# The last product of a three-stage kernel by seven products in two phases, with wider operand preparation in the stage before it

## The chip, the core and the metric

The kernel runs on one core of a Trainium2 chip. The metric is its time in microseconds of the device; the reported time is the median of three runs. The five engines of a core run programs of their own and wait for each other by semaphores: TensorE (PE) multiplies into PSUM, VectorE (DVE) and ScalarE (ACT) do elementwise work, GpSimd (POOL) has next to nothing to do here, and SyncE (SP) issues the DMA transfers.

## The reference

All values are float32. Attention without a softmax makes 4608 rows of 512, and two MLPs follow, the second with a gate:

```python
kv = einsum('bhsd,bhse->bhde', k, v); a = einsum('bhsd,bhde->bhse', q, kv)
x = a / sqrt(mean(a * a) + 1e-6) * g_norm       # 4608 x 512
h = x @ w_in                                     # 512 x 2048
x1 = (h * clip(h + 3, 0, 6) / 6) @ w_out         # 2048 x 512
g = x1 @ w_gate; val = x1 @ w_val                # 512 x 1536 each
out = (g * sigmoid(g) * val) @ w_out2            # 1536 x 512
```

## The kernel before

To keep the precision of float32, each operand of a matmul is split into a hi and a lo part (ACT copies hi, line 107; DVE subtracts to get lo, line 108), and each product is three matmuls: hi x lo, lo x hi and hi x hi. Which of the three comes first matters below: `product` (line 651) begins with the lo part of the activations.

The work comes in stages. Attention and the first MLP take the first half of the time and leave x1 in DRAM. The **gate and value stage** goes over x1 in 6 blocks of 768 tokens, twice: first with one half of the weight columns, block 0 to 5, and then with the other half, block 5 to 0. These are 12 visits, and ten times the next visit has another block. A visit has 3 steps, and a step has one quad for the gate and one for the value (`quad`), each computing a pair of column tiles for 768 tokens by seven products (a scheme of the Strassen kind) in place of eight: the activations come in as seven operands, T1, T3, B11, T2, B22, T4 and B21 in the order in which a quad uses them, B.. a quarter of the block of x and T.. a sum of quarters. Each product is 6 matmuls of 384 columns, a quad 42. The seven operands of a block are made by `prepare_x` during the last step of the visit before, from the block `xr`, loaded one visit ahead: first the sums T, then each operand's hi and lo on ACT and DVE. `gv_step` ends with the multiplication of gate and value on DVE (line 686) and a store of the result to g2d in DRAM.

Also on DVE are the sums of a quad's products (lines 668 to 677, named h1, h0 and h), which follow PE closely, since PE's accumulators in PSUM are used again. In this stage weights of later use are decoded too: w_out2 comes in as pairs of 32-bit words that `decode_w` turns into float32 (one ACT and three DVE instructions per tile), and `combine` makes the seven weight operands of a pair of tiles.

The **last product** goes over 9 blocks of 512 tokens. For each of the 12 tiles of 128 rows of w_out2 it loads a piece of g2d, splits it (`load_g2`), and multiplies it: 4 groups of 128 tokens x 3 matmuls of 512 columns (`o2_step`, lines 111 to 113). At a block's end the four accumulators are copied out and stored.

PE's program runs in the order of the code. For ACT, DVE and SP a scheduler arranges the instructions when the kernel is built; once built, each engine's sequence is fixed, and an instruction that waits holds everything behind it on its engine.

Of the kernel before, what the change touches and what calls it, by code (L numbers as in the profile page):

```python
# [18 lines left out]
def kernel(  # L19
# [579 lines left out]
    xo_slot = [0]  # L599

    def x_op(name):

        n = 6 if xo_slot[0] % 14 < 6 else 8
        pool = big["x" if n == 6 else "x2"]
        xo_slot[0] += 1
        return pool.tile([P, 2, TH], F32R, tag="xo", bufs=n, name=name)

    def prepare_x(j, x, pool=None):

        b11, b12 = x[:, 0:2, :TH], x[:, 0:2, TH:]  # L610
        b21, b22 = x[:, 2:4, :TH], x[:, 2:4, TH:]
        ops, ts = {}, {}

        def sums(*what):
            for kk in range(2):
                for key, a, b in what:
                    if pool is None or key == "T4":
                        t = w_slot(f"{key}_{j}_{kk}", F32).rearrange("p k f -> p (k f)")[:, :TH]
                    else:
                        t = pool.tile([P, TH], F32, tag="f", name=f"{key}_{j}_{kk}")  # L620
                    a_, b_ = (ts[o, kk] if isinstance(o, str) else o[:, kk] for o in (a, b))
                    nc.vector.tensor_tensor(out=t, in0=a_, in1=b_, op=ALU.subtract)
                    ts[key, kk] = t
# [406 lines left out]
```

## Time and profile before

| | |
|---|---|
| median of 3 runs | 1722.76 us (1721.68 to 1723.73) |
| profiled execution, span of its instructions | 1719.0 us |
| gate and value stage | 886.26 to 1419.56 us |
| last product | 1419.56 to 1715.0 us |
| PE busy over the span | 1688.9 us (98%) |
| DVE busy | 1185.0 us (69%) |
| ACT busy | 773.3 us (45%) |

The profile is of one execution. Its span, first to last instruction, is the part of the time that rows can be read from; the runs' times have a few microseconds more around it. A busy time is the union of an engine's instructions; a matmul's own time (0.39 us for 512 columns) is longer than the distance to the next, since they overlap, so matmuls are counted by the distance of their starts.

### The profile page before, as it was taken

The page shows a single profiled execution, that of the slowest core. Times are in us where ns is not written, and L with a number is a line of the kernel's source. Part 1 is how long each engine was busy: PE and PEld are TensorE (multiplying, and loading weights), DVE is VectorE, ACT ScalarE, POOL GpSimd, SP SyncE. Part 2 cuts the span into 40 slices and gives each one's busy share as a digit, 9 for nine tenths or more (in the row PEclk, how much of TensorE's full clock was granted, in tenths as well). Part 3 has the DMA queues.
Part 4 walks back from the last instruction along what each step waited for, and adds up shares of the span by engine and source line. Part 5 has one row for each costly group of instructions (what it writes and reads, how often), then busy time and mean ns, then how long its engine had stood idle before and what let it go on. Part 6 is the DMA issues. An engine that isn't in the chain of part 4 may idle for free.

```text
span 1719.0 us, 25593 instructions
## 1 busy us (share of the span) xinstructions
PE 1688.9 (98%) x9636; PEld 1493.1 (87%) x9636; DVE 1185.0 (69%) x2353; ACT 773.3 (45%) x1439; POOL 2.4 (0%) x7
## 2 busy tenths in 40 slices
PE   7999999999999999999999999999999999999999
PEld 3566789898898899998889999999999997888887
DVE  5897987778777777777889888777666685322321
ACT  4565554445444454545555444434443453222221
POOL 0000000000000000000000000000000000000000
PEclk8999999999999999999999999999999999999999
DMA  7886444454545444325465544572222235334332
GB/s 191 248 259 188 130 138 128 146 149 115 160 127 159 126 148 131 123 99 184 151 205 178 198 147 149 184 260 76 81 91 92 92 135 182 125 111 143 140 110 74
DMA packets 200171, 252.29 MB, mean 147 GB/s; under 512 B 79984, under 2 KB 129136, under 8 KB 200048
## 3 DMA queue, kind: packets, MB, share of 16 engines
q1 hardware_dynamic: 200048, 250.67, 45.0%
q8 instruction: 75, 1.23, 0.3%
q14 instruction: 48, 0.39, 0.1%
HBM read 185.86 MB, written 64.75 MB: 146 GB/s over the span
## 4 chain that ended last, share of the span: by engine, by line
PE 86%; DVE 8%; ACT 2%; DMA 2%; issue 1%; SPq 0%; DVEq 0%; ACTq 0%
PE q_g L651 14%; PE q_v L651 14%; PE acc L111 12%; PE acc L112 12%; PE acc L113 12%; PE a L651 6%; PE d L651 4%; PE c L651 4%; PE h L117 3%; PE kv L250 1%; DMA raw_g<-in_moe_w_gate_dram 1%; DVE lT L108 1%; DVE g L108 1%; DVE t L580 1%; PE at L112 0%
## 5 line engine op out<-in xcount | busy, mean ns | idle before, releaser
L111 PE MATMUL acc<-g,wo 128*128 128x512 f32 x512 | 202.1, 395 | 0.0
L112 PE MATMUL acc<-g,wo 128*128 128x512 f32 x512 | 199.9, 390 | 0.0
L113 PE MATMUL acc<-g,wo 128*128 128x512 f32 x512 | 199.5, 390 | 0.0
L108 DVE TENSOR_TENSOR g2l<-g,g2h 128x512 fp32r<-128x512 f32 x108 | 73.4, 692 | 139.1 <-ACT g2h L107 138.5
L111 PE MATMUL acc<-wl,g2h 128*128 128x512 f32 x432 | 168.2, 389 | 1.0 <-ACT g2h L107 1.0
L112 PE MATMUL acc<-wh,g2l 128*128 128x512 f32 x432 | 168.2, 389 | 0.3 <-DVE g2l L108 0.3
L113 PE MATMUL acc<-wh,g2h 128*128 128x512 f32 x432 | 168.1, 389 | 0.0
L579 ACT ACTIVATE t<-h,three 128x512 f32<-128x512 f32 x120 | 86.7, 722 | 138.8 <-DVE h L574 109.5
L107 ACT ACTIVATE g2h<-g 128x512 fp32r<-128x512 f32 x108 | 67.9, 632 | 147.7 <-PE acc L112 74.3
L107 ACT ACTIVATE g<-t 128x512 fp32r<-128x512 f32 x144 | 90.9, 631 | 88.8 <-DVE t L580 73.6
L108 DVE TENSOR_TENSOR g<-t,g 128x512 fp32r<-128x512 f32 x144 | 97.9, 680 | 31.6 <-ACT g L107 31.2
L113 PEld LDWEIGHTS acc<-g,wo 128*128 128x128 f32 x512 | 96.1, 188 | 20.5
L111 PEld LDWEIGHTS acc<-g,wo 128*128 128x128 f32 x512 | 96.2, 188 | 19.9
L112 PEld LDWEIGHTS acc<-g,wo 128*128 128x128 f32 x512 | 96.2, 188 | 18.3
L111 PEld LDWEIGHTS acc<-wl,g2h 128*128 128x128 f32 x432 | 81.1, 188 | 18.0 <-ACT g2h L107 1.4
L112 PEld LDWEIGHTS acc<-wh,g2l 128*128 128x128 f32 x432 | 81.1, 188 | 17.5 <-DVE g2l L108 0.6
L580 DVE SCALAR_TENSOR_TENSOR t<-t,h 128x512 f32<-128x512 f32 x120 | 82.6, 688 | 19.3 <-ACT t L579 15.7
L113 PEld LDWEIGHTS acc<-wh,g2h 128*128 128x128 f32 x432 | 81.1, 188 | 16.9
L117 PE MATMUL h<-x,w_i 128*128 128x512 f32 x192 | 87.0, 602 | 1.9 <-DVE w_i L170 1.9
L117 PEld LDWEIGHTS h<-x,w_i 128*128 128x128 f32 x192 | 36.7, 193 | 43.2 <-issue 40.2
L651 PE MATMUL q_v<-hT,v 128*128 128x384 f32 x288 | 73.6, 336 | 0.0
L679 ACT ACTIVATE hg<-q_g 128x384 f32<-128x384 f32 x36 | 17.6, 490 | 113.3 <-PE q_g L651 113.3
(245 smaller groups left out, 4483.3 us busy)
## 6 DMA issues: line engine op xcount, KB each, us to landing
wo<-wod SPq DMA_DIRECT2D x128, 512.0 KB, 3.4
g2d<-hv SPq DMA_DIRECT2D x36, 768.0 KB, 3.4
g<-g2d SPq DMA_DIRECT2D x108, 256.0 KB, 4.6
xr<-x1d SPq DMA_DIRECT2D x11, 1536.0 KB, 6.7
x1d<-x1o SPq DMA_DIRECT2D x36, 256.0 KB, 2.9
out_dram<-o SPq DMA_DIRECT2D x36, 256.0 KB, 2.1
raw_i<-in_moe_w_in_dram SPq DMA_DIRECT2D x16, 512.0 KB, 5.3
raw_o<-in_moe_w_out_dram SPq DMA_DIRECT2D x16, 512.0 KB, 4.4
```

Source lines behind the costliest of these rows:

```text
L107: nc.scalar.activation(out=hi, in_=src, func=AF.Copy)
L108: nc.vector.tensor_tensor(out=lo, in0=src, in1=f32(hi), op=ALU.subtract)
L111: nc.tensor.matmul(out_, wh, xl, start=start, stop=False)
L112: nc.tensor.matmul(out_, wl, xh, start=False, stop=False)
L113: nc.tensor.matmul(out_, wh, xh, start=False, stop=stop)
L117: nc.tensor.matmul(out_, f32(w), f32(x), start=start, stop=stop)
L250: nc.tensor.matmul(ps[h * D:(h + 1) * D, :D], kt[:, h, r, :], vt[:, h, r, :], start=i == 0, stop=i == len(steps) - 1,)
L579: nc.scalar.activation(out=t, in_=h[i], func=AF.Relu, bias=three[:, 0:1])
L580: nc.vector.scalar_tensor_tensor(out=t, in0=t, scalar=6.0, in1=h[i], op0=ALU.min, op1=ALU.mult)
L651: nc.tensor.matmul(ps, a[:, kk], b[:, kk], start=first and n == 0, stop=n == 5, skip_group_check=True,)
L679: nc.scalar.activation(out=h[:, 0], in_=a, func=AF.Copy)
```

## The change

It has three parts. The last product is now done by the scheme of seven products, too: per block of 512 tokens the 12 tiles of w_out2 make 6 pairs, and each pair needs seven products of 6 matmuls with 256 columns (`g_product`). A block has two phases: in the first (`o2_one`) all six pairs do the four products with T1, T3, B11 and T2, in the second (`o2_two`) the three with B22, T4 and B21. The operands of g2 are made for two pairs at once, in instructions of 512 and 1024 elements (`g_one` for the first phase, `g_two` for the second); B11 and B12's data are thus loaded once for the first phase, B21 and B22 twice.

The weights' seven operands per pair are made during the second half of the gate and value stage, one half pair per step in steps 18 to 29, written to DRAM and loaded again near its end.

In the gate and value stage the operands of x are prepared in wider instructions: T1, T3 and T4 each in one piece of 768 elements, B11 with T2 in one of 1536 and B21 with B22 in another. T2 is formed in place, from T3 and B11, in the block's own tile.

```diff
-    def prepare_x(j, x, pool=None):
-        b11, b12 = x[:, 0:2, :TH], x[:, 0:2, TH:]
-        b21, b22 = x[:, 2:4, :TH], x[:, 2:4, TH:]
...
-        def splits(*what):
-            for key, src in what:
-                hi, lo = x_op(f"h{key}_{j}"), x_op(f"l{key}_{j}")
-                if src is not None:
-                    split(hi, lo, src)
-                else:
-                    for kk in range(2):
-                        split(hi[:, kk], lo[:, kk], ts[key, kk])
-                ops[key] = hi, lo
-        sums(("T1", b12, b11), ("T3", b22, b12))
-        if pool is None:
-            sums(("T2", b22, "T1"), ("T4", "T2", b21))
-        splits(("T1", None), ("T3", None), ("B11", b11))
-        if pool is not None:
-            sums(("T2", b22, "T1"))
...
         yield ops
-        if pool is not None:
-            sums(("T4", "T2", b21))
-        splits(("T2", None), ("B22", b22), ("T4", None), ("B21", b21))
...
+        pair = xo_pair("x2", "B1", T2, "0")
+        for c in (slice(0, TH), slice(TH, T2)):
+            split(pair[0][:, :, c], pair[1][:, :, c], x[:, 0:2, c])
+        ops.update(halves_of(pair, "B11", "T2"))
+        yield from prepare_rest(0, x, ops)
...
+    def prepare_rest(j, x, ops):
+        t = big["xt"].tile([P, 2, TH], F32, tag="t", name=f"T4_{j}")
+        nc.vector.tensor_tensor(out=t, in0=x[:, 0:2, TH:], in1=x[:, 2:4, :TH], op=ALU.subtract)
+        pair = xo_pair("x2", "B2", T2, str(j))
+        split(pair[0], pair[1], x[:, 2:4])
+        ops.update(halves_of(pair, "B21", "B22"))
+        hi, lo = xo_pair("x", "T4", TH, str(j))
+        split(hi, lo, t)
+        ops["T4"] = hi, lo
         yield ops
+    def prepare_x(j, x):
+        ops = {}
+        b11, b12, b22 = x[:, 0:2, :TH], x[:, 0:2, TH:], x[:, 2:4, TH:]
+        t = big["xt"].tile([P, 2, TH], F32, tag="t", name=f"T1_{j}")
+        nc.vector.tensor_tensor(out=t, in0=b12, in1=b11, op=ALU.subtract)
+        nc.vector.tensor_tensor(out=b12, in0=b22, in1=b12, op=ALU.subtract)
+        for key, src in (("T1", t), ("T3", b12)):
+            hi, lo = xo_pair("x", key, TH, str(j))
+            split(hi, lo, src)
+            ops[key] = hi, lo
+        nc.vector.tensor_tensor(out=b12, in0=b12, in1=b11, op=ALU.add)
+        pair = xo_pair("x2", "B1", T2, str(j))
+        split(pair[0], pair[1], x[:, 0:2])
+        ops.update(halves_of(pair, "B11", "T2"))
+        yield from prepare_rest(j, x, ops)
...
+    def flat(o):
+        return o.rearrange("p k f -> p (k f)")
+    def w2_operands(q, tiles):
+        w2[q] = {
+            key: tuple(flat(o) for o in ops) for key, ops in operands(tiles).items()
+        }
+    def g2_rows(f0, n, r0):
+        return g2d[f0:f0 + n, :, r0:r0 + TO].rearrange("f p t -> p f t")
+    g_ops, t4s = {}, {}
...
+    def g_one(j, u):
+        n = f"{j}_{u}"
+        raw = big["gr"].tile([P, 2, 2, TO], F32, tag="raw", name=f"graw_{n}")
+        nc.sync.dma_start(
+            out=raw.rearrange("p q f t -> p (q f) t"), in_=g2_rows(4 * u, 4, j * TO)
+        )
+        t13 = big["gt"].tile([P, 2, 2, TO2], F32, tag="t13", name=f"gt13_{n}")
+        t4 = t4s[j, u] = slot(f"t4_{n}").rearrange("p (n c) -> p n c", n=2)
+        sub(
+            t13, raw[:, :, :, TO2:],
+            raw[:, :, 0].rearrange("p q (b t) -> p q b t", b=2),
+        )
+        b12 = raw[:, :, 0, TO2:]
+        sub(b12, raw[:, :, 1, TO2:], t13[:, :, 0])
+        sub(t4, b12, raw[:, :, 1, :TO2])
+        hi, lo = (
+            big["gx"].tile([P, 2, 4, TO2], F32R, tag=f"x{o}", name=f"gx{o}_{n}") for o in "hl"
+        )
+        split(hi[:, :, 0:2], lo[:, :, 0:2], t13)
+        split(
+            hi[:, :, 2:4].rearrange("p q b t -> p q (b t)"),
+            lo[:, :, 2:4].rearrange("p q b t -> p q (b t)"), raw[:, :, 0],
...
+    def g_two(j, u):
+        n = f"{j}_{u}"
+        raws_ = [slot(f"gb_{n}_{i}") for i in range(2)]
+        for i, r in enumerate(raws_):
+            nc.sync.dma_start(out=r, in_=g2d[4 * u + 2 * i + 1, :, j * TO:(j + 1) * TO])
+        hi, lo = (
+            big["gy"].tile([P, 2, 3, TO2], F32R, tag=f"y{o}", name=f"gy{o}_{n}") for o in "hl"
+        )
+        split(hi[:, :, 2], lo[:, :, 2], t4s.pop((j, u)))
+        for i, r in enumerate(raws_):
+            split(
+                hi[:, i, 0:2].rearrange("p b t -> p (b t)"),
+                lo[:, i, 0:2].rearrange("p b t -> p (b t)"), r,
+            )
...
+    def g_product(ps, g, w, first):
+        for i in range(TO2 // P):
             cs = slice(i * P, (i + 1) * P)
-            mm3(
-                ps[i], g[0][:, cs], g[1][:, cs],
-                w2[f][0].rearrange("p k f -> p (k f)"), w2[f][1].rearrange("p k f -> p (k f)"),
-                f == 0, f == NF2 - 1,
-            )
-        if f < NF2 - 1:
+            for n, (a, b) in enumerate(((g[0], w[1]), (g[1], w[0]), (g[0], w[0]))):
+                nc.tensor.matmul(
+                    ps[:, i * TO2:(i + 1) * TO2], a[:, cs], b,
+                    start=first and i == 0 and n == 0, stop=n == 2, skip_group_check=True,
+                )
...
+    def o2_one(j, q):
+        if q == 0:
+            for i, k in enumerate("aecd"):
+                acc2[k] = big["ps"].tile([P, 512], F32, tag=f"q{i}", name=f"o2{k}_{j}")
+        for k, b, a in (
+            ("c", "T1", "S1"), ("d", "T3", "S3"), ("a", "B11", "A11"), ("e", "T2", "S2"),
+        ):
+            g_product(acc2[k], g_ops.pop((j, q, b)), w2[q][a], q == 0)
+        if q < NQ - 1:
             return
...
+        acc2["u"], acc2["v"] = slot(f"u_{j}"), slot(f"v_{j}")
+        for o, p, r in (("v", "c", "d"), ("u", "a", "e")):
+            nc.scalar.activation(out=acc2[o], in_=acc2[p], func=AF.Copy)
+            nc.vector.tensor_tensor(out=acc2[o], in0=acc2[o], in1=acc2[r], op=ALU.add)
...
+    def o2_two(j, q):
+        for k, b, a in (("c", "B22", "S4"), ("d", "T4", "A22"), ("a", "B21", "A12")):
+            g_product(acc2[k], g_ops.pop((j, q, b)), w2[q][a], False)
+        if q == 0:
+            o = slot("o")
+            nc.vector.tensor_tensor(out=o, in0=acc2["u"], in1=acc2["v"], op=ALU.add)
+            put(j, o, 1, 1)
+        if q < NQ - 1:
+            return
+        for k, dm, tok in (("c", 0, 1), ("d", 1, 0)):
+            o = slot("o")
+            nc.vector.tensor_tensor(out=o, in0=acc2["u"], in1=acc2[k], op=ALU.add)
+            put(j, o, dm, tok)
+        o = slot("o")
+        nc.scalar.activation(out=o, in_=acc2["a"], func=AF.Copy)
+        put(j, o, 0, 0)
...
-                f = c - NB2 * NH
-                last = {15: (4, 5, 6), 16: (7, 8), 17: (9, 10, 11)}
-                for f in last.get(f, (f,) if f < 4 else ()):
-                    w2[f] = split_w(load_w2nd("2", f), f"2{f}")
-            if c == len(steps) - 2:
-                g2 = {m: load_g2(*order2[m]) for m in range(G_FIRST)}
...
-        for c in range(len(order2) + G_AHEAD):
-            if G_FIRST <= c < len(order2):
-                g2[c] = load_g2(*order2[c])
-            if c >= G_AHEAD:
-                j, f = order2[c - G_AHEAD]
-                if f == 0:
-                    acc2 = [
-                        big["ps"].tile([P, 512], F32, tag=f"q{i}", name=f"acc2_{j}_{i}")
-                        for i in range(TO // P)
-                    ]
-                o2_step(j, f, g2.pop(c - G_AHEAD), acc2)
...
+                m = c - NB2 * NH
+                if m < W2_STEPS:
+                    tiles = make_w2(m // 2, m % 2)
+                    if tiles:
+                        for k, t in enumerate(tiles):
+                            nc.sync.dma_start(out=w2d[m // 2, k], in_=flat(f32(t)))
+            m = c - len(steps)
+            if m == -3:
+                reload_w2(0)
+                g_first(JO[0], 0)
+            elif m == -2:
+                reload_w2(1)
+                g_first(JO[0], 1)
+            elif m == -1:
+                reload_w2(2)
+                reload_w2(3)
...
+        units = [(j, h, u) for j in JO for h in range(2) for u in range(NQ // 2)]
+        def prepare_g(n):
+            if 0 < n < len(units):
+                j, h, u = units[n]
+                (g_two if h else g_one)(j, u)
+        prepare_g(1)
+        reload_w2(4)
+        reload_w2(5)
+        for n, (j, h, u) in enumerate(units):
+            prepare_g(n + 2)
+            for q in (2 * u, 2 * u + 1):
+                (o2_two if h else o2_one)(j, q)
 
```

The first place is the change of blocks in the gate and value stage on DVE: here block 3 is made ready during the last value quad of block 2's first visit. lT, lB are the lo parts of the sums T and of the quarters B, hv the value quad's result, the xr and T rows in the second fence the sums T2 and T4. Before, from the quad's first sum on:

```order
L668 TENSOR_TENSOR h1v_11280<-h1v_11280,q_v_11284 128x384
L108 TENSOR_TENSOR lT_3_11354<-T_3_0_11337,hT_3_11353 128x384
L108 TENSOR_TENSOR lT_3_11354<-T_3_1_11341,hT_3_11353 128x384
L108 TENSOR_TENSOR lT_3_11360<-T_3_0_11339,hT_3_11359 128x384
L672 TENSOR_TENSOR h0v_11279<-h0v_11279,q_v_11282 128x384
L108 TENSOR_TENSOR lT_3_11360<-T_3_1_11343,hT_3_11359 128x384
L675 TENSOR_TENSOR hv_11278<-h1v_11280,h0v_11279 128x384
L676 TENSOR_TENSOR hv_11278<-h0v_11279,q_v_11283 128x384
L108 TENSOR_TENSOR lB_3_11366<-xr_10942,hB_3_11365 128x768
L677 TENSOR_TENSOR hv_11278<-h0v_11279,q_v_11284 128x384
L108 TENSOR_TENSOR lT_3_11370<-T_3_0_11345,hT_3_11369 128x384
L686 TENSOR_TENSOR hv_11278<-hg_11220,hv_11278 128x1536
```

The same place after the change:

```order
L691 TENSOR_TENSOR h1v_11219<-h1v_11219,q_v_11223 128x384
L110 TENSOR_TENSOR lT_3_11280<-T_3_11276,hT_3_11279 128x768
L110 TENSOR_TENSOR lT_3_11284<-xr_10881,hT_3_11283 128x768
L695 TENSOR_TENSOR h0v_11218<-h0v_11218,q_v_11221 128x384
L664 TENSOR_TENSOR xr_10881<-xr_10881 128x2x384
L698 TENSOR_TENSOR hv_11217<-h1v_11219,h0v_11218 128x384
L699 TENSOR_TENSOR hv_11217<-h0v_11218,q_v_11222 128x384
L700 TENSOR_TENSOR hv_11217<-h0v_11218,q_v_11223 128x384
L644 TENSOR_TENSOR T_3_11292<-xr_10881 128x768
L709 TENSOR_TENSOR hv_11217<-hg_11159,hv_11217 128x1536
L110 TENSOR_TENSOR lB_3_11289<-xr_10881,hB_3_11288 128x1536
L110 TENSOR_TENSOR lB_3_11295<-xr_10881,hB_3_11294 128x1536
```

The lo part of B11 stood between two of the quad's sums and ahead of the multiplication; the lo of B11 and T2, now one instruction of 1536 elements, stands behind T2's sum, T4's sum and the multiplication. (Two pairs of lB follow each other in this piece of the program; the first is B11 with T2.)

On ACT at the same place the hi parts (hT, hB) are made, between copies of accumulators (h1v, h0v, hv). Before:

```order
L667 ACTIVATE h1v_11280<-q_v_11283 128x384
L107 ACTIVATE hT_3_11353<-T_3_0_11337 128x384
L107 ACTIVATE hT_3_11353<-T_3_1_11341 128x384
L107 ACTIVATE hT_3_11359<-T_3_0_11339 128x384
L670 ACTIVATE h0v_11279<-q_v_11281 128x384
L107 ACTIVATE hT_3_11359<-T_3_1_11343 128x384
L107 ACTIVATE hB_3_11365<-xr_10942 128x768
```

After:

```order
L690 ACTIVATE h1v_11219<-q_v_11222 128x384
L109 ACTIVATE hT_3_11279<-T_3_11276 128x768
L109 ACTIVATE hT_3_11283<-xr_10881 128x768
L693 ACTIVATE h0v_11218<-q_v_11220 128x384
L109 ACTIVATE hB_3_11288<-xr_10881 128x1536
L702 ACTIVATE hv_11217<-q_v_11220 128x384
L109 ACTIVATE hB_3_11294<-xr_10881 128x1536
```

Four hi parts of 384 elements became two of 768, and B11's copy of 768 elements became one of 1536 that needs T2's sum from DVE.

On PE a block of the last product begins as follows, acc being the four accumulators and g2h, g2l the split rows of g2. Before:

```order
L111 MATMUL acc_4_0_16229<-wl_12866,g2h_0_16069 128x512
L112 MATMUL acc_4_0_16229<-wh_12865,g2l_0_16070 128x512
L113 MATMUL acc_4_0_16229<-wh_12865,g2h_0_16069 128x512
L111 MATMUL acc_4_1_16230<-wl_12866,g2h_0_16069 128x512
L112 MATMUL acc_4_1_16230<-wh_12865,g2l_0_16070 128x512
L113 MATMUL acc_4_1_16230<-wh_12865,g2h_0_16069 128x512
```

After (o2c is one of four accumulators, gxh and gxl hold the operands of two pairs):

```order
L815 MATMUL o2c_16311<-20_3_14867,gxh_0_16196 128x256
L815 MATMUL o2c_16311<-20_2_14866,gxl_0_16197 128x256
L815 MATMUL o2c_16311<-20_2_14866,gxh_0_16196 128x256
L815 MATMUL o2c_16311<-20_3_14867,gxh_0_16196 128x256
L815 MATMUL o2c_16311<-20_2_14866,gxl_0_16197 128x256
L815 MATMUL o2c_16311<-20_2_14866,gxh_0_16196 128x256
```

The matmuls have half the columns, and a group of six belongs to one of the seven products.

## Rows read from the trace of the kernel before

**Rows 1.** The page, its first part: busy us (share) xinstructions of each engine.

```profile
PE 1688.9 (98%) x9636; PEld 1493.1 (87%) x9636; DVE 1185.0 (69%) x2353; ACT 773.3 (45%) x1439; POOL 2.4 (0%) x7
```

**Rows 2.** Windows of the two stages: length, busy us (x) by engine, clock, DMA.

```profile
886.26:1419.56 533.30, 531.96 (x3026) 527.39 (x3024) 415.41 (x732) 243.32 (x429) 0.00 (x0) 1.00 0.40 144
1419.56:1715.00 295.44, 294.18 (x1297) 242.98 (x1296) 90.92 (x134) 79.84 (x129) 0.00 (x0) 1.00 0.36 125
```

**Rows 3.** Timeline of PE, last product: start us, us, engine, line, operation.

```profile
1450.22 0.39 PE L112 MATMUL acc<-wh,g2l 128*128 128x512 f32 x1
...
1454.98 0.39 PE L112 MATMUL acc<-wh,g2l 128*128 128x512 f32 x1
```

**Rows 4.** Timeline of PE, 256-column products of the first MLP.

```profile
406.67 0.28 PE L651 MATMUL a<-lB,wh_i 128*128 128x256 f32 x1
...
410.87 0.28 PE L651 MATMUL a<-hB,wh_i 128*128 128x256 f32 x1
```

**Rows 5.** The page's costliest groups: splits in the last product on DVE.

```profile
L108 DVE TENSOR_TENSOR g2l<-g,g2h 128x512 fp32r<-128x512 f32 x108 | 73.4, 692 | 139.1 <-ACT g2h L107 138.5
```

**Rows 6.** Timeline of DVE at a change of blocks.

```profile
1193.67 0.56 DVE L668 TENSOR_TENSOR h1v<-h1v,q_v 128x384 f32<-128x384 f32 x1 [2.90 <-ACT h1v L667]
...
1197.42 0.95 DVE L108 TENSOR_TENSOR lB<-xr,hB 128x768 fp32r<-128x768 f32 x1
1198.29 0.55 DVE L677 TENSOR_TENSOR hv<-h0v,q_v 128x384 f32<-128x384 f32 x1
1198.75 0.55 DVE L108 TENSOR_TENSOR lT<-T,hT 128x384 fp32r<-128x384 f32 x1
1199.22 1.75 DVE L686 TENSOR_TENSOR hv<-hg,hv 128x1536 f32<-128x1536 f32 x1
1200.89 0.55 DVE L108 TENSOR_TENSOR lT<-T,hT 128x384 fp32r<-128x384 f32 x1
```

**Rows 7.** Windows: a step of the gate and value stage without preparation.

```profile
1228.00:1242.60 14.60, 14.60 (x85) 14.60 (x84) 9.05 (x16) 7.42 (x14) 0.00 (x0) 1.00 0.14 55
```

**Rows 8.** Timeline of PE at the same change of blocks.

```profile
1191.06 0.34 PE L651 MATMUL q_v<-lT,v 128*128 128x384 f32 x1
...
1198.39 0.34 PE L651 MATMUL q_g<-lT,wh_g 128*128 128x384 f32 x1
...
1200.51 0.34 PE L651 MATMUL q_g<-lB,wh_g 128*128 128x384 f32 x1
```

**Rows 9.** Timeline of ACT at the same change of blocks.

```profile
1191.78 1.49 ACT L684 ACTIVATE hg<-hg 128x1536 f32<-128x1536 f32 x1
1193.17 0.47 ACT L667 ACTIVATE h1v<-q_v 128x384 f32<-128x384 f32 x1
...
1195.57 0.84 ACT L107 ACTIVATE hB<-xr 128x768 fp32r<-128x768 f32 x1
```

**Rows 10.** Waits of PE in the gate and value stage: us, times, longest.

```profile
PE q_v L651 <- ACT h1v L667: 0.8, 1, 0.8
```

**Rows 11.** Timeline of PE at three pauses, and windows behind them.

```profile
24.03 2.04 PE L117 MATMUL at<-qhi,kv 128*128 128x512 f32 x2 [2.12 <-DVE kv L257]
...
46.42 0.51 PE L111 MATMUL acc<-g,wh_o 128*128 128x512 f32 x1 [2.26 <-ACT wh_o L107]
...
47.87 0.63 PE L111 MATMUL acc<-g,wh_o 128*128 128x512 f32 x1
...
50.86 0.43 PE L112 MATMUL acc<-g,wl_o 128*128 128x512 f32 x1
...
819.31 0.38 PE L651 MATMUL d<-lT,n_i 128*128 128x256 f32 x1 [1.71 <-DVE v L569]
...
23.70:33.70 10.00, 7.05 (x8) 2.23 (x9) 5.67 (x10) 4.30 (x8) 0.00 (x0) 0.50 0.41 105
...
47.50:50.90 3.40, 3.40 (x10) 2.62 (x9) 2.63 (x5) 1.60 (x3) 0.00 (x0) 0.50 0.69 195
...
819.40:829.00 9.60, 9.60 (x59) 8.65 (x60) 9.50 (x20) 5.09 (x11) 0.00 (x0) 1.00 0.47 170
```

More of the change, by code (lines that the diff above doesn't have):

```diff
@@ L71 @@
     TO = 512
+    TO2 = TO // 2
     NP1 = NF // 2
@@ L597, in load_x1, with xo_pair @@
         return x
[L599 to L606, printed above, removed]
-    def prepare_x(j, x, pool=None):
-        b11, b12 = x[:, 0:2, :TH], x[:, 0:2, TH:]
-        b21, b22 = x[:, 2:4, :TH], x[:, 2:4, TH:]
+    def xo_pair(pool, tag, width, name):
+        return [
+            big[pool].tile([P, 2, width], F32R, tag=f"{o}{tag}", name=f"{o}{tag}_{name}")
+            for o in "hl"
+        ]
@@ L612, in prepare_x, with halves_of, prepare_first @@
+    def halves_of(pair, low, high):
+        return {
+            low: tuple(o[:, :, :TH] for o in pair), high: tuple(o[:, :, TH:] for o in pair),
+        }
+    def prepare_first(x):
         ops, ts = {}, {}
-        def sums(*what):
+        for key, r0, c0 in (("T1", 0, 0), ("T3", 2, TH)):
             for kk in range(2):
-                for key, a, b in what:
-                    if pool is None or key == "T4":
-                        t = w_slot(f"{key}_{j}_{kk}", F32).rearrange("p k f -> p (k f)")[:, :TH]
-                    else:
[L620 to L623, printed above, removed]
@@ new lines, in prepare_first @@
+                nc.vector.tensor_tensor(out=t, in0=a_, in1=b_, op=ALU.subtract)
+        for key in ("T1", "T3"):
+            hi, lo = xo_pair("x", key, TH, "0")
+            for kk in range(2):
+                split(hi[:, kk], lo[:, kk], ts[key, kk])
+            ops[key] = hi, lo
+        for kk in range(2):
+            nc.vector.tensor_tensor(
+                out=x[:, kk, TH:], in0=ts["T3", kk], in1=x[:, kk, :TH], op=ALU.add
+            )
+        yield ops
+        pair = xo_pair("x2", "B1", T2, "0")
@@ new lines, in g_first @@
+    def g_first(j, q):
+        n = f"{j}_{q}"
+        ra, rb, t13 = slot(f"ra_{n}"), slot(f"rb_{n}"), slot(f"t13_{n}")
+        for i, r in enumerate((ra, rb)):
+            nc.sync.dma_start(out=r, in_=g2d[2 * q + i, :, j * TO:(j + 1) * TO])
+        if q % 2 == 0:
+            t4s[j, q // 2] = slot(f"t4_{n}").rearrange("p (n c) -> p n c", n=2)
+        sub(t13[:, :TO2], ra[:, TO2:], ra[:, :TO2])
+        sub(t13[:, TO2:], rb[:, TO2:], ra[:, TO2:])
+        sub(ra[:, TO2:], rb[:, TO2:], t13[:, :TO2])
+        sub(t4s[j, q // 2][:, q % 2], ra[:, TO2:], rb[:, :TO2])
+        for keys, src in ((("T1", "T3"), t13), (("B11", "T2"), ra)):
+            hi, lo = slot(f"gh_{n}", F32R), slot(f"gl_{n}", F32R)
+            split(hi, lo, src)
+            for i, key in enumerate(keys):
+                g_ops[j, q, key] = tuple(o[:, i * TO2:(i + 1) * TO2] for o in (hi, lo))
@@ new lines, in g_two @@
+    def g_two(j, u):
[5 more added lines that the diff above has]
+            big["gy"].tile([P, 2, 3, TO2], F32R, tag=f"y{o}", name=f"gy{o}_{n}") for o in "hl"
+        )
+        split(hi[:, :, 2], lo[:, :, 2], t4s.pop((j, u)))
[3 more added lines that the diff above has]
+                lo[:, i, 0:2].rearrange("p b t -> p (b t)"), r,
+            )
+        for i in range(2):
+            for k, key in enumerate(("B21", "B22", "T4")):
+                g_ops[j, 2 * u + i, key] = hi[:, i, k], lo[:, i, k]
@@ new lines, in put @@
+    def put(j, o, dm, tok):
+        r0 = j * TO + tok * TO2
+        nc.sync.dma_start(
+            out=out[r0:r0 + TO2, dm * TO2:(dm + 1) * TO2].rearrange("(s p) c -> p s c", p=P),
+            in_=o.rearrange("p (s c) -> p s c", c=TO2),
+        )
+    def o2_two(j, q):
[14 more added lines that the diff above has]
+        put(j, o, 0, 0)
@@ L947, with make_w2, reload_w2 @@
         ready.clear()
-        order2 = [(j, f) for j in reversed(range(NT // TO)) for f in range(NF2)]
-        G_AHEAD = 8
-        G_FIRST = 3
+        JO = list(reversed(range(NT // TO)))
+        W2_STEPS = 2 * NQ
+        w2_half = {}
+        def make_w2(q, half):
+            w2_half[half] = load_w2_pair(q, half)
+            if half:
+                return combine([w2_half.pop(0), w2_half.pop(1)], f"2{q}")
+        def reload_w2(q):
+            tiles = [w_slot(f"2{q}_{i}", F32R) for i in range(7)]
+            for i in (2, 3, 4, 5, 0, 1, 6):
+                nc.sync.dma_start(out=flat(f32(tiles[i])), in_=w2d[q, i])
+            w2_operands(q, tiles)
         for c, (n, j, p) in enumerate(steps):
```

69 lines of the change are left out of this document (43 added, 26 removed).

## The prediction

> **What bounds the kernel now.** I read the page first: TensorE (PE) is busy 1688.9 us, 98% of the 1719.0 us span, so time is gained only by taking work from it and lost by making it wait [rows 1]. The windows then split the two stages that the change touches: the gate and value stage (886.26 to 1419.56 us) has PE busy 531.96 of 533.30 us and VectorE (DVE) 415.41; the last product (1419.56 to 1715.00) has PE 294.18 of 295.44 and DVE only 90.92 [rows 2]. So in the last product PE alone is the limit, with DVE two thirds idle, while in the gate and value stage DVE has more to do and stands close behind PE. The profiled execution lasted 1719.0 us; the median of the runs is 1722.76, 3.8 us more, which I leave as it is: I sum differences and put them on the median.
>
> **Last product.** It removes 9 blocks x 12 rows x 4 x 3 = 1296 matmuls of 512 columns and adds 9 x 6 pairs x 7 products x 6 = 2268 of 256. In the stage's steady part 21 steps of the 512-column matmul take from 1450.22 to 1454.98 us, 226.7 ns each [rows 3]. The stage has no 256-column ones, but the products of the first MLP have: 35 steps from 406.67 to 410.87 us, 120.0 ns, each with its own 128x128 weight load, as here [rows 4]. That is 1296 x 0.2267 = 293.8 us against 2268 x 0.1200 = 272.2 us: 21.6 us less. The 1.3 us that PE isn't busy in this stage [rows 2] go if the new operands come early, so −22.9 us.
>
> Do they come early? Per block PE has 252 matmuls, 30.2 us. DVE has nine instructions of 1024 elements and twenty of 512. A 512-element split takes 0.69 us [rows 5]; one of 1536 takes 1.75 and one of 768 takes 0.95 [rows 6], so 1024 is about 1.2. That is at most 9 x 1.2 + 20 x 0.69 = 24.6 us under 30.2 us of PE. DMA reads grow by half where its share is 0.36 [rows 2]. Both are covered; were DVE the limit it would have to be 1.2 times slower than these rows. At the stage's end PE is followed by one copy and its store before and by one sum and its store after: nothing.
>
> [...]
>
> **Preparing w_out2's seven operands in the gate and value stage.** Before, the second half of that stage decoded and split twelve weight tiles; now it decodes twelve and combines six pairs, over steps 18 to 29. Per pair the decodes are six DVE instructions and the combination eight, 256 or 512 elements, none over 0.69 us: below 14 x 0.69 = 9.7 us per two steps, 4.8 us a step. A step with no preparation has DVE busy 9.05 of 14.60 us [rows 7]: with it 13.9. Cost nothing on the path, covered by PE, 0.7 us to spare; were that cover gone, each such step would be its excess longer. The seven operands go to DRAM and come back (2 x 11 MB) where DMA is at a share of 0.14 [rows 7], in SP's queue behind the x load. I take 0, up to 3 us if a reload is late for the first block.
>
> **Visit changes: the wider operand preparation.** This decides. Ten times the stage changes to another block of x. The next block's operands are split while the last v quad runs. I set that quad's start (1191.06 in the change shown) as 0; the next g quad starts at 7.33 us and reaches B11, its lo part first, at 1200.51, 9.45 us [rows 8]. Before, B11's lo is made at 1197.42 (6.36 to 7.31 us), ahead of the multiplication hv, 2 us before PE comes [rows 6]. What the changes lose now is bounded by the stage: a quad's 42 matmuls start within 7.33 us, 0.1745 each [rows 8], and 72 quads x 7.33 = 527.8 us, 5.5 less than the stage's 533.30 [rows 2]. Its start takes a part of these (0.8 us are one wait [rows 10]); I put 3.7 on the ten changes.
>
> After, by the order of instructions, B11 lies in a pair with T2, 1536 wide, and T2 needs T3's lo done. DVE's sequence is h1v, lT1, lT3, h0v, T2, three hv sums, T4, hv multiplication, and only then lB1. With starts spaced as rows show (384 elements 0.47, 768 0.87, 1536 1.67 [rows 6]; ACT's 768-wide copy lasts 0.84, its 1536-wide one 1.49 [rows 9]) the times are: h1v 2.61 as now; lT1 3.35 (ACT's half is made behind its h1v copy and ends there); lT3 4.22; h0v 5.09; T2 5.56 to 6.51; hv sums 6.43, 6.90, 7.37; T4 7.84 to 8.79; multiplication 8.71 to 10.46; lB1 10.37 to 12.12. ACT's half of B1 runs 6.55 to 8.04 and the copy hv behind it to 8.42, so neither holds the multiplication. PE wants lB1 at 9.45: it waits 2.7 us, and 2.8 with the start of a matmul. Queued behind lB1 on DVE stand lB2 (12.0 to 13.8) and lT4 (14.6); with PE late these are in time (B22 is then wanted at 14.4). So the stall is paid once per change. Six of ten changes have this sequence: 17.0 us. At two (first half j = 2, second half j = 4) ACT makes B2's hi before B1's, and lB1 comes 0.45 us later: 3.3 each, 6.6. At two more (j = 1 and second half j = 3) DVE also does lB2 before lB1: 12.26 to 14.01 us, 4.7 each, 9.5. Sum 33.1 less the 3.7 of now: **+29.4 us**. From below: if the rows' spacings overlap better by one 768-wide instruction, 0.87 us less each, +20.7; from above, one more such instruction in front, +38.
>
> **Start of the stage.** The first pair's hi and lo stand ahead of g_14's on ACT and DVE, in memory that MLP1's tiles hold until PE has read them. Price: one 1536-wide copy ahead of what PE waits for, 1.49 us [rows 9], less some 0.5 of the 0.8 us wait that stands in the first step now [rows 10]: +1, from 0 to 3.
>
> **TensorE's clock.** [...] A pause of 1.71 us at 819.31 had 1.00 behind it [rows 11]. [...]
>
> **Sum.** −22.9 + 29.4 + 1 + 11 = +18.5: 1722.76 + 18.5 = 1741.
>
> **Rivals.**
> - *Stalls without the clock's fall*: −22.9 + 29.4 + 1 = +7.5, 1730. [...]
> - *lB1 isn't late (faster)*: DVE's queue reaches lB1 before PE does. It decides from a mean stall of 2.56 us per change (ten of them less 3.7, plus 1, equal 22.9). My mean is 3.3, so 0.75 us per change is the margin, less than one 768-wide instruction. With no stall at all it is −22.9 − 3.7 + 1 = −25.6, 1697; with half the stalls −9, 1714. Against it: in the trace DVE does exactly the order's sequence, with no idle time in it.
> - *The balance*: stalls 0.87 us shorter and no clock fall: −22.9 + 20.7 + 1, −1.2, 1721.6: no change.
> - *The last product gains nothing*, its operands late at each of the 18 phases by 1.3 us, 23 us in all; with the stalls 1764. Against it: DVE's 24.6 under 30.2.
>
> **How the numbers follow.** A difference of 0.2% (3.4 us) is what a measurement of this kernel can tell from none. Chances: stalls with clock falls, 1734 to 1748, 0.50; without, 1727 to 1733, 0.20; balance 0.08; faster 0.15; last product late, 0.07. Slower 0.77, same 0.08, faster 0.15. The range leaves out most of the faster case and of the last: 1716 to 1752. The likeliest case alone, 1734 to 1748.
>
> **What would show it.** After: the last stage about 272 us long, PE busy throughout, 256-column matmuls 0.12 us apart. In the gate and value stage ten PE waits for the DVE line that makes lB (line 110), 2.7 to 4.8 us each, the two longest at the change to j = 1 in the first half and to j = 3 in the second; granted clock 0.50 for a few us behind most. Steps 18 to 29 without PE waits outside the changes. Wrong if lB1 is done before PE comes, if PE waits inside the last product, or if the last product's matmuls keep another pitch.

## The result, and the profile after

The changed kernel takes 1747.16 us (median of 4 runs, 1742.88 to 1749.35) where the one before takes 1722.22 (1720.95 to 1723.73) beside it: a ratio of 1.0147, 95% interval 1.013 to 1.0164. It is 24.9 us slower; forecast were 18.5 us, and 1741 us with a range of 1716 to 1752.

The page after (busy us and share of the span; then the group with the largest wait: its count, busy time, mean ns of one, idle time before it and what ended that):

```profile
PE 1685.5 (97%) x10608; PEld 1539.0 (88%) x10608; DVE 1316.7 (75%) x2427; ACT 806.7 (46%) x1426; POOL 2.4 (0%) x7
...
L674 PE MATMUL q_g<-lB,wh_g 128*128 128x384 f32 x192 | 72.9, 380 | 30.2 <-DVE lB L110 30.2
```

PE is busy 3.4 us less than in [rows 1], though the span grew from 1719.0 to 1746.5 us. One group of matmuls, those that begin the product with B11 in a gate quad, now waits 30.2 us for lB on DVE. The windows of the two stages (length, busy us of PE, PEld, DVE, ACT, POOL, then clock, DMA share, GB/s):

```profile
886.89:1467.36 580.47, 549.00 (x3025) 544.76 (x3024) 435.20 (x688) 243.21 (x385) 0.00 (x0) 0.96 0.49 174
1467.36:1742.20 274.84, 273.49 (x2269) 272.41 (x2268) 203.34 (x254) 111.86 (x160) 0.00 (x0) 1.00 0.53 179
```

Beside [rows 2] the gate and value stage grew from 533.30 to 580.47 us (+47.2), and the last product shrank from 295.44 to 274.84 us (−20.6). The start of the gate and value stage moved from 886.26 to 886.89, and 0.2 us came at the end: +47.2 − 20.6 + 0.6 + 0.2 = +27.4 us, the difference of the two profiled spans.

The waits of PE in the gate and value stage (us in total, times, longest):

```profile
PE q_g L674 <- DVE lB L110: 30.2, 10, 4.5
PE q_v L674 <- ACT h1v L690: 0.5, 1, 0.5
PE q_v L674 <- DVE h1v L691: 0.4, 1, 0.4
PE q_g L674 <- DVE h1g L691: 0.3, 1, 0.3
```

Nearly all of it is lB, ten times. The timeline of DVE at the change to block 3 in the first half (start, duration; the view joins like neighbours as x2):

```profile
1028.55 0.55 DVE L691 TENSOR_TENSOR h1v<-h1v,q_v 128x384 f32<-128x384 f32 x1 [2.90 <-ACT h1v L690]
...
1031.49 0.95 DVE L664 TENSOR_TENSOR xr<-xr 128x768 f32<-128x768 f32 x1
1032.36 0.55 DVE L698 TENSOR_TENSOR hv<-h1v,h0v 128x384 f32<-128x384 f32 x1
...
1033.76 0.95 DVE L644 TENSOR_TENSOR T<-xr 128x768 f32<-128x768 f32 x1
1034.63 1.75 DVE L709 TENSOR_TENSOR hv<-hg,hv 128x1536 f32<-128x1536 f32 x1
1036.30 3.42 DVE L110 TENSOR_TENSOR lB<-xr,hB 128x1536 fp32r<-128x1536 f32 x2
1039.63 0.95 DVE L110 TENSOR_TENSOR lT<-T,hT 128x768 fp32r<-128x768 f32 x1
```

The timeline of PE in the same stretch, the g quad's first matmul and the first with B11's lo:

```profile
1033.28 0.34 PE L674 MATMUL q_g<-lT,wh_g 128*128 128x384 f32 x1
...
1038.10 0.45 PE L674 MATMUL q_g<-lB,wh_g 128*128 128x384 f32 x1 [2.55 <-DVE lB L110]
```

This is the sequence that the order of instructions gave: T2's sum at 1031.49, three hv sums, T4's sum at 1033.76, the multiplication at 1034.63, and B11's lo with T2's from 1036.30. With the g quad at 1033.28 as 7.33, lB1 starts at 10.35 (predicted 10.37) and PE waits 2.55 us. What comes on top is the clock. Windows behind three of the ten pauses:

```profile
988.70:994.00 5.30, 5.30 (x17) 5.30 (x18) 3.93 (x6) 0.49 (x1) 0.00 (x0) 0.50 0.42 110
1038.20:1041.60 3.40, 3.40 (x12) 3.40 (x13) 2.85 (x3) 0.49 (x1) 0.00 (x0) 0.58 0.56 144
1425.40:1428.80 3.40, 3.40 (x20) 3.40 (x21) 3.37 (x5) 0.49 (x1) 0.00 (x0) 1.00 0.50 145
```

Behind the pauses that end at 988.63 and 1038.10 the granted clock is 0.50 and, on the mean of the window, 0.58; behind that which ends at 1425.31, also 2.55 us long, it is 1.00. Over the whole stage the clock is 0.96 on average where it was 1.00. What that costs is read from PE's steps at 0.50, here behind the first of these pauses:

```profile
989.12 0.53 PE L674 MATMUL q_g<-hB,wl_g 128*128 128x384 f32 x1
...
993.92 0.53 PE L674 MATMUL q_g<-hB,wl_g 128*128 128x384 f32 x1
```

These are 15 steps of 0.320 us, where a step at 1.00 takes 0.1745. The stage has 41.0 us at 0.50 in nine stretches, and PE is busy in 37.0 us of them (a stretch can begin before the pause ends): 37.0 x (1 − 0.1745 / 0.320) = 17 us lost. The pauses themselves cost 31.9 us by the starts of the matmuls; the 30.2 us of waits are less, since each is counted from the end of the matmul before it, 0.16 us after the next could have started. So +47.2 is 31.9 of pauses, less the 3.7 that the changes lost before, and 17 of clock; the remaining 2 us are in small losses that were not followed up. The runs themselves differ by the clock: the one of 1742.88 us had a mean clock of 0.989, that of 1749.35 us 0.985.

The last product in its steady part (first and last of 35 steps):

```profile
1599.81 0.28 PE L815 MATMUL o2e<-23_3_15178,gxh 128*128 128x256 f32 x1
...
1604.01 0.28 PE L815 MATMUL o2c<-25_2_15237,gxh 128*128 128x256 f32 x1
```

That is 120.0 ns a step, the figure from [rows 4].

### The profile page after: what moved, and what is told of

The parts are those of the page before. It is cut to its first block, busy times and chain, and to the rows that moved or that the text cites. A ratio compares the mean times of both kernels' runs of the same rounds, so it can differ in the third digit from the quotient of the medians.

```text
span 1746.5 us, 27728 instructions
## 1 busy us (share of the span) xinstructions
PE 1685.5 (97%) x10608; PEld 1539.0 (88%) x10608; DVE 1316.7 (75%) x2427; ACT 806.7 (46%) x1426; POOL 2.4 (0%) x7
## 4 chain that ended last, share of the span: by engine, by line
PE 72%; DVE 14%; DMA 6%; ACT 3%; issue 3%; SPq 1%; DVEq 0%; ACTq 0%
PE q_g L674 15%; PE q_v L674 14%; PE acc L113 7%; PE acc L114 6%; PE acc L115 6%; PE a L674 6%; PE d L674 4%; PE c L674 4%; PE h L119 3%; DMA gb<-g2d 2%; DMA graw<-g2d 2%; DVE gxl L110 2%; DVE lB L110 1%; PE o2d L815 1%; PE o2a L815 1%
## 5 line engine op out<-in xcount | busy, mean ns | idle before, releaser
L115 PEld LDWEIGHTS acc<-g,wo 128*128 128x128 f32 x512 | 96.1, 188 | 20.6
L674 PE MATMUL q_g<-lB,wh_g 128*128 128x384 f32 x192 | 72.9, 380 | 30.2 <-DVE lB L110 30.2
L702 ACT ACTIVATE hg<-q_g 128x384 f32<-128x384 f32 x36 | 17.7, 491 | 132.4 <-PE q_g L674 128.7
L674 PE MATMUL q_v<-hB,v 128*128 128x384 f32 x288 | 73.2, 335 | 0.0
L709 DVE TENSOR_TENSOR hv<-hg,hv 128x1536 f32<-128x1536 f32 x36 | 63.2, 1754 | 13.0 <-ACT hv L702 12.7
L674 PE MATMUL q_g<-hB,wl_g 128*128 128x384 f32 x192 | 71.5, 372 | 0.0
L674 PEld LDWEIGHTS q_g<-lB,wh_g 128*128 128x128 f32 x192 | 41.5, 216 | 33.5 <-DVE lB L110 33.5
L674 PE MATMUL q_g<-hB,wh_g 128*128 128x384 f32 x192 | 70.9, 369 | 0.0
L691 DVE TENSOR_TENSOR h1v<-h1v,q_v 128x384 f32<-128x384 f32 x36 | 19.9, 553 | 65.1 <-ACT h1v L690 65.1
L674 PE MATMUL a<-lB,wh_i 128*128 128x256 f32 x240 | 68.2, 284 | 0.0
L674 PE MATMUL a<-hB,wh_i 128*128 128x256 f32 x240 | 67.9, 283 | 0.0
```

The costliest lines, as they stand in the source:

```text
L115: nc.tensor.matmul(out_, wh, xh, start=False, stop=stop)
L674: nc.tensor.matmul(ps, a[:, kk], b[:, kk], start=first and n == 0, stop=n == 5, skip_group_check=True,)
L691: nc.vector.tensor_tensor(out=v, in0=v, in1=d, op=ALU.add)
L709: nc.vector.tensor_tensor(out=hv, in0=hg, in1=hv, op=ALU.mult)
```

## The experiments

**1. The new last product without the wide preparation.** The changed kernel with the old functions for x's operands and their tiles:

```diff
-    def prepare_first(x):
-    def prepare_rest(j, x, ops):
-    def prepare_x(j, x):
+    def prepare_x(j, x, pool=None):
...
-                        parts = prepare_first(x1)
+                        parts = prepare_x(0, x1, fpool)
```

> The new last product and its weight preparation, with the old operand preparation of x. Theory A (the wide preparation of x makes the whole loss, by B11's lo coming late at ten changes of blocks and by the clock behind these pauses; the last product itself gains 21 us, 295.8 to 274.8): no wait of PE for lB over 0.5 us, clock 1.00 through the gate and value stage, which keeps its 533 us, and 1722 - 21 = 1701 us (1698 to 1705). Rival B (the extra weight preparation in steps 18 to 29 has a part in the loss: DVE is fuller there): waits of PE in these steps and 1706 us or more.

Measured: 1703.74 us, a ratio of 0.9901 (0.9886 to 0.9915) to the kernel before. Waits of PE from the gate and value stage's start to past the last product's first change of phase:

```profile
PE o2c L795 <- ACT v L815: 2.2, 1, 2.2
PE q_v L654 <- ACT h1v L670: 0.8, 1, 0.8
PE o2d L795 <- DVE v L816: 0.8, 1, 0.8
```

Two windows of the same run, the gate and value stage and the stretch behind that pause:

```profile
886.00:1419.16 533.16, 532.00 (x3025) 527.44 (x3024) 439.61 (x789) 251.13 (x447) 0.00 (x0) 1.00 0.52 185
1438.80:1445.60 6.80, 6.04 (x30) 5.83 (x31) 6.43 (x9) 1.36 (x2) 0.00 (x0) 0.57 0.37 112
```

In ten changes there is no wait for lB, and the stage takes 533.16 us, with PE busy 532.00 of them, as before [rows 2]. So the weight preparation in steps 18 to 29 is hidden as forecast: rival B is out. What is left is a pause at the first change of phase in the last product, with a clock of 0.57 behind it.

**2. The wide preparation without the new last product.** The kernel before with the three new functions, the tile for T1 and T4, and the raw weight tile given back earlier to make room:

```diff
-    def prepare_x(j, x, pool=None):
+    def prepare_first(x):
+    def prepare_rest(j, x, ops):
+    def prepare_x(j, x):
...
+        big["xt"] = ctx.enter_context(tc.tile_pool(name="xt", bufs=1, reuse_waits="tile"))
```

> The old last product with the wide preparation of x. Theory A: waits for lB of 2.5 to 4.5 us at ten changes, some 29 us together, less 3.7 that the changes lose now, and 17 to 20 us by a clock of 0.50 behind nearly all of them: 1722 + 25 + 18 = 1765 us (1758 to 1772). Rival B (a part of the loss needs the new weight preparation beside it): under 1752 us.

Measured: 1762.46 us beside 1721.46 (ratio 1.0233, 1.0216 to 1.025), +41.0 us. The waits:

```profile
PE q_g L671 <- DVE lB L108: 27.9, 10, 4.5
```

27.9 less 3.7 is 24 us, and 26 by the starts of the matmuls; PE is busy for 31.7 us at a clock of 0.50, which by the reading above costs another 14. The loss is there without the new weight preparation. The two parts of the change nearly add up: −17.7 (first run) and +41.0 make +23.3, the whole change is +24.9. That they come so close is in part chance. The gate and value stage grows by 43.2 us here (533.30 to 576.52) and by 47.3 beside the new last product (533.16 to 580.47), with a little more of waits and of clock, while the first run loses some 5 us by the pause in its last product, which the changed kernel doesn't have (279.4 against 274.84 us).

**3. A pause made shorter by work.** One more product in the first gate quad after a change, into the accumulator that the next product clears:

```diff
         product(d, w["S3"], xo["T3"], True)
+        if fill:
+            product(a, w["S1"], xo["T1"], True)
```

> The changed kernel with one product more (12 matmuls of 384 columns, T1 by S1 into the accumulator that the next product clears, so nothing of the result changes) in the first gate quad after each change of blocks, between T3's product and B11's. It makes PE work 2.1 us more at each change and shortens the pause to 0.5 us at six changes, 0.9 at two and 2.4 at two; lB comes at the same time as before. Theory A with the clock as a cost of its own: the clock stays at 1.00 behind eight changes or more, and the time falls by 8 falls x some 2 us, to 1731 us (1727 to 1736), with more work. Rival C (the clock's fall costs nothing beside the pauses, since PE would wait for DVE anyway): 1747 us, as the changed kernel.

The expectation has the size of the edit wrong: a product is 6 matmuls, 1.05 us, and not 12. Measured: 1733.13 us (ratio 1.0066, 1.0051 to 1.0081), 14 us less than the changed kernel's 1747.16, with 60 matmuls more to do. The waits for lB:

```profile
PE q_g L674 <- DVE lB L110: 19.7, 10, 3.4
```

Windows of this run behind pauses of 1.95, 1.50 and 1.96 us:

```profile
990.30:993.20 2.90, 2.90 (x11) 2.90 (x10) 2.49 (x3) 0.49 (x1) 0.00 (x0) 0.50 0.24 31
1038.40:1041.80 3.40, 3.40 (x20) 3.40 (x21) 3.37 (x5) 0.49 (x1) 0.00 (x0) 1.00 0.53 144
1223.60:1227.00 3.40, 3.40 (x21) 3.40 (x21) 3.40 (x5) 1.01 (x2) 0.00 (x0) 1.00 0.27 33
```

The waits fell by 30.2 − 19.7 = 10.5 us, which is just the 10 x 1.05 us put in: lB came no earlier. Still 14 us were gained. In the profiled executions 10.8 us of this lie in the gate and value stage (580.47 to 569.70), where PE is busy at 0.50 for 12.4 us in place of 37.0: that is the clock, and rival C is out. Another 2.7 us lie in the last product, which in this execution has no waits for v; why is not shown. All six pauses of 1.5 us have 1.00 behind them, and of two equal ones, 1.95 and 1.96 us, one has 0.50 and the other 1.00.

**4. B11 apart from T2.**

```diff
-        nc.vector.tensor_tensor(out=b12, in0=b12, in1=b11, op=ALU.add)
         pair = xo_pair("x2", "B1", T2, str(j))
-        split(pair[0], pair[1], x[:, 0:2])
+        split(pair[0][:, :, :TH], pair[1][:, :, :TH], b11)
+        nc.vector.tensor_tensor(out=b12, in0=b12, in1=b11, op=ALU.add)
+        split(pair[0][:, :, TH:], pair[1][:, :, TH:], b12)
```

> The changed kernel with B11's hi and lo as instructions of 768 elements of their own, ahead of T2's sum; all else stays wide. By the order of instructions B11's lo then stands ahead of the multiplication at all ten changes, but T2's lo stands behind the 1536-wide lo of B21 and B22 at four (j = 1 and 2 in the first half, 4 and 3 in the second). Theory A (the place of one lo in DVE's sequence decides, not the width as such): no wait at six changes, some 2 us each at four, perhaps a fall of the clock behind these: 1701 + 5 + up to 8 = 1710 us (1703 to 1716). Rival D (the wide instructions as such are slow for this stage, whatever is first): 1735 us or more.

Measured: 1733.98 us (ratio 1.0075, 1.0057 to 1.0093). It is 13 us better than the changed kernel, and 24 us worse than theory A said. Three rows of PE at the change to block 3, the first matmuls of the products with B11, T2 and B22:

```profile
1032.51 0.34 PE L675 MATMUL q_g<-lB,wh_g 128*128 128x384 f32 x1
...
1034.42 0.44 PE L675 MATMUL q_g<-lB,wh_g 128*128 128x384 f32 x1 [0.70 <-DVE lB L110]
...
1037.05 0.42 PE L675 MATMUL q_g<-lB,wh_g 128*128 128x384 f32 x1 [1.30 <-DVE lB L110]
```

B11 comes in time (1032.51, no wait). But T2's lo is 0.70 us late and B22's 1.30 us: together 2.0 where the changed kernel had 2.55. Six changes are like this, and at the other four PE waits 2.6 to 2.8 us: 22.8 us for lB in all, where theory A had 8. With PE held up at B11, T2 and B22 had only looked punctual. Theory A falls in the form that the place of one lo decides.

**5. All sums early, the pairs still wide.** T3 and T4 get tiles of their own, so that no sum waits for T3's lo:

```diff
-        nc.vector.tensor_tensor(out=b12, in0=b22, in1=b12, op=ALU.subtract)
+        t3 = [half("T3", kk) for kk in range(2)]
+        for kk in range(2):
+            sub2(t3[kk], b22[:, kk], b12[:, kk])
+        sub2(b12, b22, t1)
+        t4 = [half("T4", kk) for kk in range(2)]
+        for kk in range(2):
+            sub2(t4[kk], b12[:, kk], b21[:, kk])
...
-        nc.vector.tensor_tensor(out=b12, in0=b12, in1=b11, op=ALU.add)
```

> The changed kernel with the wide pairs kept (B11 with T2, B21 with B22, 1536 elements each, T1 in 768), but T3 and T4 in tiles of their own in halves of 384, so that all four sums are made before the last value quad and none waits for T3's lo. By the order of instructions lB1 then stands ahead of the multiplication and lB2 behind it. Theory A2 (what decides is how much DVE work stands ahead of B22's lo, which PE wants 24 matmuls into the next quad; T2's and T4's sums in the sequence, 1.7 us, and B21 bundled with B22, 0.9 us, are the lateness): waits of 0.3 to 1 us per change, no fall of the clock, 1701 to 1708 us. Rival D (1536-wide splits as such are too long for this place): waits of 2 us or more per change, 1720 us or more.

Measured: 1708.96 us (ratio 0.9938, 0.9921 to 0.9956), 1 us over theory A2's range. The waits for lB:

```profile
PE q_g L694 <- DVE lB L110: 5.9, 10, 0.8
```

The window of this run's gate and value stage, to be read beside experiment 1's, and DVE at the change to block 3:

```profile
886.80:1428.53 541.73, 534.52 (x3026) 527.43 (x3024) 435.16 (x728) 247.61 (x405) 0.00 (x0) 1.00 0.52 185
...
1022.79 1.75 DVE L110 TENSOR_TENSOR lB<-xr,hB 128x1536 fp32r<-128x1536 f32 x1
1024.45 1.75 DVE L729 TENSOR_TENSOR hv<-hg,hv 128x1536 f32<-128x1536 f32 x1
1026.12 1.75 DVE L110 TENSOR_TENSOR lB<-xr,hB 128x1536 fp32r<-128x1536 f32 x1
```

Ten waits of 0.8 us at most, 5.9 us in all; the clock stays at 1.00 through the stage. No sum stands between the lo of B11 with T2 (1022.79) and that of B21 with B22 (1026.12) any more. Rival D is out: the splits of 1536 elements are still there. What they save is a little of DVE's time: over the stage DVE is busy 435.16 us in 728 instructions where experiment 1, narrow, has 439.61 in 789. But experiment 1's stage is 8.6 us shorter. In a stage that PE bounds, 4.5 us less of DVE are worth nothing, and an operand that is 0.6 us late at each change costs that and a little more.

**6. All operands apart, T2 still in place.** Experiment 4 with B22 split alone, then T4's sum and split, then B21:

```diff
-        yield from prepare_rest(j, x, ops)
+        pair = xo_pair("x2", "B2", T2, str(j))
+        split(pair[0][:, :, TH:], pair[1][:, :, TH:], b22)
+        t = big["xt"].tile([P, 2, TH], F32, tag="t", name=f"T4_{j}")
+        nc.vector.tensor_tensor(out=t, in0=b12, in1=x[:, 2:4, :TH], op=ALU.subtract)
+        hi, lo = xo_pair("x", "T4", TH, str(j))
+        split(hi, lo, t)
+        ops["T4"] = hi, lo
+        split(pair[0][:, :, :TH], pair[1][:, :, :TH], x[:, 2:4, :TH])
...
```

> The kernel of the fourth run (B11 apart from T2) with B22 and B21 apart as well, T4's sum behind B22; T2 is still made in place behind T3's lo. Theory A2: six changes lose 0.7 to 0.9 us (T2's lo behind the multiplication), the other four, where T2's sum itself stands behind the multiplication, some 2 us; no wait for B22; the clock falls at most behind the four: 1703 to 1715 us, 20 us or more under the fourth run's 1734. Rival E (DVE's work in the whole last step, not its order, is too much): no better than 1728 us.

Measured: 1730.73 us (ratio 1.0055, 1.0039 to 1.0071): 3 us better than experiment 4, not 20, and so within what rival E allowed. At a change in the first half PE waits for T2's lo, and then for T4's:

```profile
1032.89 0.44 PE L684 MATMUL q_g<-lB,wh_g 128*128 128x384 f32 x1 [0.71 <-DVE lB L110]
...
1036.83 0.44 PE L684 MATMUL q_g<-lT,n_g 128*128 128x384 f32 x1 [1.56 <-DVE lT L110]
```

The timeline of DVE there:

```profile
1029.34 0.95 DVE L666 TENSOR_TENSOR xr<-xr 128x768 f32<-128x768 f32 x1
1030.21 1.75 DVE L719 TENSOR_TENSOR hv<-hg,hv 128x1536 f32<-128x1536 f32 x1
1031.88 1.82 DVE L110 TENSOR_TENSOR lB<-xr,hB 128x768 fp32r<-128x768 f32 x2
1033.62 0.95 DVE L672 TENSOR_TENSOR T<-xr 128x768 f32<-128x768 f32 x1
1034.48 0.95 DVE L110 TENSOR_TENSOR lB<-xr,hB 128x768 fp32r<-128x768 f32 x1
1035.35 0.55 DVE L701 TENSOR_TENSOR h1g<-h1g,q_g 128x384 f32<-128x384 f32 x1
1035.82 0.95 DVE L110 TENSOR_TENSOR lT<-T,hT 128x768 fp32r<-128x768 f32 x1
```

DVE has no pause between T2's sum (1029.34) and T4's lo (1035.82). T2's sum and T4's sum (1033.62) take 0.87 us each in this row of work, and whichever operand stands last is late by them. So it isn't the bundling of early with late operands that costs most, as theory A2's second half had it, but the two sums that T2's place in T3's tile forces behind T3's lo. In experiment 5 they are out of the row, and the waits for lo parts in the stage are 5.9 us where they are 24.4 here (15.0 for lB, 9.4 for lT). This also answers rival E: DVE is busy 435.15 us in this run's stage and 435.16 in experiment 5's, so it is the order and not the amount. Four kernels show the two effects side by side. With the sums in the row PE waits 30.2 us for lo parts when the pairs are wide (the changed kernel) and 24.4 when the operands are apart (here); with the sums early it waits 5.9 us when they are wide (experiment 5), and in the old narrow preparation not at all (experiment 1).

**7 and 8. The pause in the last product.** Experiment 1's ACT in front of that pause:

```profile
1434.96 1.30 ACT L109 ACTIVATE gyh<-gb 128x512 fp32r<-128x512 f32 x2 [7.61 <-DMA gb<-g2d]
1436.17 1.04 ACT L109 ACTIVATE gxh<-gt 128x1024 fp32r<-128x1024 f32 x1
1437.12 1.13 ACT L109 ACTIVATE gyh<-gb 128x512 fp32r<-128x512 f32 x2
1438.15 0.57 ACT L815 ACTIVATE v<-o2c 128x512 f32<-128x512 f32 x1
```

ACT had waited 7.61 us for rows of g2, and the copy v<-c, for which PE waits, stood behind five hi copies (x2 is two of them). Run 7 issues a unit's operands (a unit is two pairs in one phase) behind the products at the end of each phase:

```diff
-            prepare_g(n + 2)
+            if u < NQ // 2 - 1:
+                prepare_g(n + 2)
             for q in (2 * u, 2 * u + 1):
                 (o2_two if h else o2_one)(j, q)
+            if u == NQ // 2 - 1:
+                prepare_g(n + 2)
```

> The first run's kernel (new last product, old preparation of x), with the operands of the unit after next issued behind the products at the end of each phase, so that fewer hi copies that wait for a transfer stand ahead of the copy v<-c on ACT. There PE had its one long pause of that run (2.2 and 0.8 us at the first change of phase) and 6.8 us at a clock of 0.50 behind it, about 3.4 us lost. Theory F (ACT's queue holds v<-c behind copies that wait for DMA): the pause 1.1 us shorter or gone, no fall of the clock, 1697 to 1701 us. Rival G (the transfers themselves are late and PE waits for the operands instead): 1702 to 1706 us.

Measured: 1712.03 us (ratio 0.9948, 0.993 to 0.9966), slower than experiment 1 and outside what both F and G said.

```profile
PE o2c L795 <- ACT v L815: 5.5, 6, 2.3
PE o2d L795 <- DVE v L816: 3.8, 8, 0.6
```

The same wait now comes at six changes of phase, up to 2.3 us. Theory F is not borne out: a later issue of the operands makes the copy no earlier. Why it is late at the other changes was not followed up. Run 8 changes the place of the transfers instead:

```diff
         prepare_g(1)
         reload_w2(4)
+        prepare_g(2)
+        prepare_g(3)
         reload_w2(5)
...
-            prepare_g(n + 2)
+            if n > 1:
+                prepare_g(n + 2)
```

> The first run's kernel (new last product, old preparation of x) with the rows of g2 for the second phase of the first block, and for its last unit, issued on SP ahead of the seven reloads of the last weight pair. In the first run DVE and ACT stood idle 4.6 and 7.6 us for these rows, and v<-c was copied late behind them: a pause of 2.2 and 0.8 us on PE and 6.8 us at a clock of 0.50. Theory G (the transfers are late by their place in SP's queue): no pause over 1 us at the first change of phase, no fall of the clock, 1698 to 1701 us. Rival H (DMA's rate in this stretch is the limit, whatever goes first): the pause moves to another tile, 1702 to 1706 us.

Run 9, beside it, is experiment 1's kernel again:

> The first run's kernel once more, beside the one before it, on the same chip: 1702 to 1706 us, with the pause at the first change of phase.

Measured on one chip: 1700.29 us with the rows first (ratio 0.9878, 0.9865 to 0.9892), 1702.91 us for experiment 1's kernel again (0.9901, 0.9886 to 0.9916). All of PE's waits from the start of the gate and value stage to the end, in run 8:

```profile
PE q_v L654 <- ACT h1v L670: 0.8, 1, 0.8
```

The last product's window in run 8:

```profile
1419.89:1693.31 273.42, 273.04 (x2268) 272.22 (x2268) 203.30 (x254) 112.36 (x160) 0.00 (x0) 1.00 0.55 189
```

PE is busy 273.04 of 273.42 us, at a clock of 1.00. Theory G holds, and run 8 is the best version here: 20.6 us faster than the kernel before.

## Why the prediction was right

The direction and the mechanism were right, step by step; of the 6 us between 1741 and 1747 the clock's term is the most.
- *Last product*: −22.9 forecast, −20.6 measured. The step of 120.0 ns is exact; in the profiled run 1.35 us of PE stay unused, 1.2 of them waits for v at changes of phase, which the sum had at nothing; PE waiting inside the last product was one of the prediction's signs of being wrong, and it came true by this much. Run 8, without them, has −22.0 on the windows (273.42 against 295.44).
- *Weight preparation*: 0 forecast; in experiment 1 the stage takes 533.16 us where it took 533.30, though DVE is busy 24.2 us more (439.61 against 415.41).
- *Changes of blocks*: stalls of 2.8, 3.3 and 4.7 us forecast, 2.55, 3.00 and 4.47 shown as waits, at the changes that were named; six, two and two of them. The forecast counted starts of matmuls, and by these the stalls are 2.7, 3.2 and 4.6 us: 33.1 forecast, 31.9 measured.
- *Start of the stage*: +1 forecast. The stage begins 0.6 us later, but in the runs with the old preparation (1, 7, 8 and 9) it begins anywhere from 885.70 to 887.11 us, so this term is not shown.
- *Clock*: this is the term that was mis-sized, 11 us forecast and 17 measured. The 11 us were the author's estimate, seven falls of the clock at 1.6 us each, worked out from the second window of [rows 11], 3.4 us at 0.50, and its steps; no run shows this term. In its place the changed kernel showed a fall behind nine of ten pauses, and three of these lasted longer than 3.4 us: at 988.70 the clock is 0.50 for 5.3 us and more. Experiment 3 shows some 11 us of it without any change in when lB comes. The seven was a choice between none and all ten, not worked out; that the term came within 6 us is in part luck.

Where the explanation was thinner than the sum: the prediction named lB1's place as the loss. Experiments 4 and 6 show that the next operand is late as soon as lB1 isn't; the loss is DVE's whole row of work between T3's lo and T4's lo, grown by T2's and T4's sums.
